# Two transposed loads on TensorE, six on-chip transposes, a shorter root, and a new instruction order in a one-core SSM + MLP kernel

## The chip, the cores and the metric

The kernel runs on one core of a Trainium2 chip. A core has five engines with an instruction queue each: TensorE (PE, matmuls; its weight loads are listed as PEld), VectorE (DVE), ScalarE (ACT), GpSimd (POOL) and SyncE (SP, which here only issues transfers). Transfers can be issued from SP, ACT and POOL; 16 DMA engines carry them. Operands lie in on-chip memory of 128 partitions; TensorE writes its results to a separate memory, PSUM, from which ACT or DVE must copy them out ("evacuate") before the space can be used again. The metric is device time in microseconds (us), the median of several runs.

## What is computed

Two layers, each an SSM convolution (A) and an MLP (B), on a sequence of 2048 tokens of 512 channels in bfloat16. Cut from the reference:

```
def _A_ref(q, k, v, shift_k, ssm_k, ssm_D):
    k_shift = causal convolution of k with 4 taps per channel (shift_k: 512 x 4)
    kv = k_shift * v
    y = causal convolution of kv with ssm_k over the sequence (FFT of length 2 S)
    return q * (y + kv * ssm_D)

def _B_ref(x, w1, b1, w2, b2):
    h = gelu(layernorm(x) @ w1 + b1)          # 512 -> 1376
    return h @ w2 + b2                        # 1376 -> 512

x = A_q
for layer in range(2):
    x = x + _A_ref(layernorm(x), A_k, A_v, A_shift_k, A_ssm_k, A_ssm_D)
    x = x + _B_ref(layernorm(x), B_w1, B_b1, B_w2, B_b2)
```

A's inputs k and v don't depend on x, so y is computed once and serves both layers.

## The kernel before

The sequence is cut into four groups of 512 tokens (j or g = 0 to 3). The convolution over the sequence is done blockwise in a transformed domain, all by matmuls with tables: K{j} is the transform of the filter's block j, U{j} that of kv's block j, and output block j is the inverse transform of the sum over a of U{a} times K{j-a}.

Work is cut into pieces, each added to a plan with a name and an engine. Two strings written out by hand fix everything: `ORDER` lists all pieces, each with its engine (S = SP, A = ACT, D = DVE, G = POOL, P0 to P3 = PE writing PSUM buffer 0 to 3), and the pieces of an engine stand in its queue in that order; `PLACE` gives each buffer its address in one large tile, `arena`, and four `zone` tiles. The names that matter below:

- Loads (line 324): lK{j} the filter's block, lk{j}, lv{j}, lx{j} the blocks of k, v and q, lT0 to lT3 the tables of the direct transform, lY the last table, ls the taps, lD the vector ssm_D, lb the bias b1, w1 and w2, w3, w4 the weights and b2. 
- KT{j} and kt{j} (lines 381, 402): 16 transposes on PE of the filter's or k's block, for j = 0 in two halves; KT00e is the evacuation of KT00, and so for all names with an e at their end. dt (line 386, DVE) adds ssm_D to the filter's first row.
- dg (line 362, DVE): turns the taps into 16 diagonal 64-wide matrices, with which kv{j}{h} (line 422) makes the 4-tap convolution on PE; kvm (line 433) multiplies it by v.
- KD, UD (line 459): the direct transform of blocks 0 and 1, eight matmuls of 128x512 each. KS and KW, US and UW (lines 484 and 493): the same for blocks 2 and 3 in two steps, with a regrouping through DMAs (Kx, Ux) between them. T (line 515, DVE): the products U times K. V, Vx, Y (lines 528, 324, 541): the inverse transform, again with a regrouping by DMA.
- For each layer l and group g, i = 2g + l: sa, pa, aa are the first norm's statistics (DVE, lines 274 to 281), root (POOL, lines 284 to 289) and application (ACT, line 294, or DVE, line 296); ga the gate and residual (lines 606 and 607); sb, pb, ab the second norm; then the normalized rows are transposed for the first product m1 (line 634, PE), whose result goes through the gelu ge (line 641, ACT), and m2 (line 652, PE) with its residual re (line 658, DVE) ends the layer; st (line 666) stores.

The transpose between ab and m1 has three ways: i = 0 goes through PE (LT, line 592); i = 7 by four DMA transposes that read on-chip memory (line 598, one per 128 tokens); all others write the rows to DRAM (dw, line 324, to a tensor `lnd`), and one DMA transpose reads them back (line 622).

The taps, the bias and ssm_D are loaded from POOL's queue: the taps as 512 pieces of four elements, the bias one element to a partition (lines 557 and 558), so that they land with channels in partitions.

In the built program every transfer of SP and ACT signals its landing on one of eight semaphores, DMAHW0 to DMAHW7, which are handed out in turn. A transfer that gets a semaphore for the second time waits before it is issued until the earlier transfer with that semaphore has landed.

Of the kernel before, what the change touches and what calls it, by code (L numbers as in the profile page):

```python
# [9 lines left out]
BF16 = mybir.dt.bfloat16  # L10
# [11 lines left out]
UD03e.A KD11.P0 aa22.D kt10e.A T001.D V00.P2 KD13.P1 KD11e.D V00e.A ke2.G ke3.G lF.A T002.D V01.P3 kv20.P2 V01e.A T003.D
V02.P0 kv21.P3 Vx01.S kvm20.D V02e.A Vx00.S V03.P0 kvm21.D kv10.P2 V03e.A Vx02.S US21.P3 kvm10.D KT20.P0 US21e.A Vx03.S
KD13e.D US20.P2 kv11.P3 ks100.S US20e.A KT20e.D US23.P1 Ux21.A KD12.P2 ks101.S kvm11.D US23e.A Ux20.S Y00.P0 US22.P3
KD12e.D Y00e.A KS22.P1 Ux23.S UD11.P2 US22e.A ga00.D KS22e.A Ux22.S T100.D Y01.P0 UD10.P3 Y01e.A ks110.S UD11e.A UD12.P1
ga02.D ks111.S UD10e.A sb00.D lK3.S UW23.P0 w1.S KS21.P2 UD12e.A UD13.P3 T110.D UW23e.A pb00.G KS21e.A on0.G UW20.P1
KS23.P0 UD13e.A UW20e.D KS20.P2 KS23e.A ab00.D UW21.P3 UW22.P1 KS20e.A sb02.D KT30.P0 UW22e.A Kx20.S V11.P2 KT30e.D
pb02.G UW21e.A LT00.P1 Kx22.S T101.D V10.P0 LT00e.A Kx21.S KS30.P3 V11e.A KS33.P1 V10e.A Kx23.S T111.D KS32.P2 KS30e.A
Vx11.S KS31.P0 KS33e.A ab02.D V13.P3 Vx10.S KS32e.A KS31e.D V12.P1 V13e.A LT02.P2 V12e.D KW23.P0 Vx13.S LT02e.A KW20.P3
T210.D KW22.P1 KW20e.A m103.P2 Vx12.S KW23e.A lk3.S KW21.P3 KW22e.D m105.P0 ge03.A w2.S KW21e.D m100.P1 ge05.A T221.D  # L30
ks201.S Y11.P2 Y10.P0 ge00.A m104.P3 ks200.S Y10e.A Y11e.D Kx32.S m101.P1 ge04.A T220.D Kx31.S m102.P0 ge01.A ga20.D
kt30.P2 ge02.A m200.P3 sb20.D Kx30.S Kx33.S kt30e.D pb20.G T200.D m202.P1 ab22.A ab20.A dw22.S re00.D T201.D dw20.S
V20.P0 T211.D V21.P2 V20e.A dr2.S kv31.P3 V21e.A re02.D KW31.P0 KW32.P2 KW31e.A lv3.S sa10.D V22.P1 KW32e.A V23.P0
sa12.D pa10.G V22e.A KW30.P2 m121.P1 on2.G V23e.D KW30e.A pa12.G aa10.A kvm31.D Vx23.S m125.P2 kv30.P0 aa12.D Vx21.S
ge25.A KW33.P3 ge21.A m122.P2 kvm30.D Vx20.S KW33e.A ga10.D US31.P1 Vx22.S ge22.A m124.P0 US31e.A sb10.D m120.P3 ge24.A
Ux31.S Y21.P2 ks300.S Y20.P1 ge20.A m123.P0 Y20e.D pb10.G Y21e.A US33.P3 ge23.A US30.P2 ab10.D US32.P1 ab12.D dw10.S
US32e.A m222.P0 ga40.D dw12.S US33e.A Ux32.S US30e.A Ux33.S sb40.D dr1.S m220.P1 T321.D Ux30.S pb40.G ks301.S ab42.A
T320.D ab40.A dw42.S m114.P3 re20.D dw40.S m113.P2 lx3.S ge14.A re22.D UW33.P1 m112.P3 T310.D ge13.A UW33e.A dr4.S
UW31.P0 m115.P2 sa32.D UW31e.A m110.P1 ge15.A T311.D ge12.A pa32.G UW30.P0 m111.P2 ge10.A sa30.D UW30e.A m145.P3 UW32.P1
m140.P0 ge45.A T301.D pa30.G UW32e.A m144.P3 aa30.A T331.D ge40.A m141.P1 ge11.A T300.D m142.P0 ge41.A V32.P2 T330.D  # L40
aa32.A V33.P1 V32e.A sa60.D ge44.A V31.P2 V33e.A V30.P3 ge42.A Vx33.S ga30.D pa60.G Vx32.S on1.G m143.P1 V30e.A on4.G
aa60.D V31e.A Vx30.S aa62.D m212.P0 sb30.D Vx31.A ge43.A pb30.G Y31.P3 Y30.P2 re12.D m240.P1 Y31e.A ab30.D Y30e.D ab32.D
ga60.D dw32.S dw30.S m210.P0 sb60.D dr3.S m242.P3 pb60.G re10.D st12.S on6.G ab62.A ab60.D dw62.S dw60.S m133.P2 re42.D
re40.D m135.P0 ge33.A m134.P3 dr6.S sa50.D m132.P1 sa52.D ge34.A pa50.G st10.S m131.P2 aa50.A pa52.G ge32.A m163.P3
aa52.D ga52.D ge35.A m165.P1 ge63.A ga50.D m130.P0 ge31.A sb50.D m164.P3 ge30.A sb52.D pb50.G ge65.A m161.P2 on3.G
pb52.G m162.P0 ge61.A ab52.D ge64.A m160.P1 ab50.D dw52.S dw50.S ge62.A m230.P2 ge60.A dr5.S m262.P3 re30.D st30.A
# [9 lines left out]
TD3:720 Dc:64 DG:1544 Ktok0:0 Ktok1:352 Ktok2:496 Ktok3:304 kT0:312 kT1:48 kT2:312 kT3:1158 K0:998 K1:560 K2:0 ziK2:1416
zsK20:16 zsK21:0 zsK22:336 zsK23:1528 K3:304 ziK3:1416 zsK30:416 zsK31:1319 zsK32:1335 zsK33:368 U0:1255 U1:1191 U2:432
ziU2:1352 zsU20:216 zsU21:0 zsU22:312 zsU23:16 U3:216 ziU3:1416 zsU30:1335 zsU31:934 zsU32:720 zsU33:736 ziV0:1416
T000:816 vs00:480 T001:0 vs01:280 T002:216 vs02:32 T003:416 vs03:264 y0:1576 x0:784 ziV1:1352 T100:32 T110:934 vs10:1560
vs11:1480 T101:720 T111:32 vs12:966 vs13:982 y1:496 x1:688 ziV2:1352 T200:1352 T210:304 T220:1480 vs20:1560 vs21:1335  # L60
# [642 lines left out]
```

## Time and profile before

| | us |
|---|---|
| median of 3 runs | 256.19 (254.76, 256.19, 256.83) |
| the profiled execution | 255.47 |
| its span, first to last instruction | 253.8 |
| DVE busy | 178.4 (70%) |
| ACT busy | 141.3 (56%) |
| POOL busy | 46.3 (18%) |

All times below come from that one profiled execution. Busy time is the time in which an engine has at least one instruction under way. In lists of groups, "x16" is the count of instructions; in a timeline a row is a run of like instructions, with the start, the time from the first's start to the last's end, and in square brackets how long the engine had been idle before it and what ended that. "SPq" and "ACTq" are the queues' own instructions, such as the issue of a transfer. Six of the eight DMA transposes of the MLP stage are those of line 622; one more group of four is line 598's.

### The profile page before, as it was taken

How to read it: one execution, taken by the hardware profiler on the slowest of the kernel's cores; microseconds unless marked ns; L12 is line 12 of the kernel's file. 1: busy time of each engine (PE TensorE's matmuls, PEld its weight loads, DVE VectorE, ACT ScalarE, POOL GpSimd, SP SyncE). 2: the span in 40 equal slices, each digit the busy share in tenths (PEclk: the TensorE clock that was granted, in tenths of full speed). 3: DMA queues.
4: the chain of work that ended last, by engine and by line, in shares of the span. 5: the costliest groups of instructions: out<-in, count | busy, mean ns of one | idle time of the engine just before them, and what ended most of it. 6: DMA issues, size and time to landing. Idle time of an engine off the chain costs nothing.

```text
span 253.8 us, 4351 instructions
## 1 busy us (share of the span) xinstructions
PE 240.5 (95%) x1675; PEld 115.4 (45%) x1675; DVE 178.4 (70%) x282; ACT 141.3 (56%) x184; POOL 46.3 (18%) x81
## 2 busy tenths in 40 slices
PE   2599999999999999999999999999999999999994
PEld 2354646434444545444444454444444444444452
DVE  0369898898999989899997995975870249630033
ACT  2428786679986347886298974121776044605400
POOL 7051300004000101210726041030230013300000
PEclk9999999999999999999999999999999999999999
DMA  6999954777669995466963015256205100211113
GB/s 195 232 259 284 295 166 112 201 194 301 189 155 302 182 209 129 147 164 182 212 187 63 3 30 140 83 124 164 45 18 147 41 3 1 53 30 41 44 31 94
DMA packets 37173, 34.59 MB, mean 136 GB/s; under 512 B 17408, under 2 KB 32896, under 8 KB 36896
## 3 DMA queue, kind: packets, MB, share of 16 engines
q1 hardware_dynamic: 34928, 32.06, 48.6%
q10 hardware_dynamic: 1904, 1.89, 3.1%
q0 software_dynamic: 320, 0.37, 0.7%
q8 instruction: 13, 0.21, 0.3%
q14 instruction: 8, 0.07, 0.1%
HBM read 12.80 MB, written 5.24 MB: 71 GB/s over the span
## 4 chain that ended last, share of the span: by engine, by line
PE 76%; DMA 8%; DVE 7%; POOL 3%; issue 2%; SPq 2%; ACT 2%; DVEq 0%; POOLq 0%
PE p L634 27%; PE p L652 23%; PE p L459 11%; PE p L528 6%; DMA zone<-arena 5%; PE p L484 3%; DMA arena<-in_A_ssm_D_dram 3%; SPq L324 2%; PE p L541 2%; PE p L493 1%; PE p L422 1%; DVE arena L658 1%; DVE arena L515 1%; DVE lst L274 1%; DVE arena L257 1%
## 5 line engine op out<-in xcount | busy, mean ns | idle before, releaser
L634 PE MATMUL p<-arena 128*128 128x512 bf16 (+1 forms) x352 | 78.9, 379 | 0.3 <-ACT arena L641 0.3
L652 PE MATMUL p<-arena 128*128 128x512 bf16 (+2 forms) x363 | 77.4, 372 | 0.1
L641 ACT ACTIVATE arena<-p,B 128x512 bf16<-128x512 f32 (+1 forms) x88 | 54.2, 684 | 41.0 <-PE p L634 39.7
L255 ACT ACTIVATE arena<-p 128x1024 bf16<-128x1024 f32 (+2 forms) x59 | 60.2, 1053 | 25.9 <-PE p L459 7.8
L284 POOL TENSOR_TENSOR lrs<-lrs,mhalf 128x2 f32<-128x2 f32 (+1 forms) x24 | 24.4, 1018 | 162.9 <-DVE lrs L278 86.4
L652 PEld LDWEIGHTS <-arena 128*128 128x128 bf16 (+1 forms) x363 | 35.3, 98 | 41.0 <-issue 0.8
L634 PEld LDWEIGHTS <-arena 128*128 128x128 bf16 (+1 forms) x352 | 34.4, 100 | 41.8 <-issue 3.5
L658 DVE TENSOR_TENSOR arena<-p,arena 128x1024 bf16<-128x1024 f32 (+2 forms) x19 | 19.8, 1053 | 46.4 <-PE p L652 46.4
L274 DVE BATCH_NORM_STATS2 lst<-arena 128x6 f32<-128x512 bf16 x64 | 40.2, 680 | 0.3
L515 DVE TENSOR_TENSOR arena<-arena 128x4096 bf16<-128x4096 bf16 (+1 forms) x16 | 32.0, 2017 | 1.4 <-ACT arena L255 1.2
L459 PE MATMUL p<-arena 128*128 128x512 bf16 x128 | 30.8, 395 | 0.5 <-DVE arena L386 0.5
L294 ACT ACTIVATE arena<-arena,lnm,lrs 128x512 bf16<-128x512 bf16 x24 | 18.0, 804 | 21.9 <-POOL lnm L289 21.9
L459 PEld LDWEIGHTS <-arena 128*128 128x128 bf16 x128 | 12.5, 101 | 16.5 <-issue 3.7
L528 PE MATMUL p<-arena,Mt 64*64 64x512 bf16 x224 | 14.9, 380 | 0.5 <-DVE arena L658 0.4
L515 DVE TENSOR_TENSOR zone<-arena 128x4096 bf16<-128x4096 bf16 x6 | 13.6, 2284 | 1.4 <-DMA zone<-arena 1.4
L296 DVE TENSOR_SCALAR arena<-arena,lmv,lrs 128x512 bf16<-128x512 bf16 x32 | 12.0, 424 | 2.5 <-POOL lrs L284 2.5
L528 PEld LDWEIGHTS <-Mt 64*64 64x64 bf16 x320 | 9.0, 106 | 8.9 <-issue 1.9
L257 DVE CAST arena<-p 128x1024 bf16<-128x1024 f32 x9 | 10.9, 1219 | 2.1 <-PE p L493 0.7
L257 DVE COPY arena<-p 128x2048 bf16<-128x2048 bf16 (+1 forms) x5 | 5.6, 1114 | 8.1 <-PE p L381 8.1
L381 PE MATMUL p<-IDt,arena 128*128 128x128 bf16 x64 | 5.1, 242 | 5.1 <-DMA arena<-in_A_ssm_k_dram 5.1
L484 PE MATMUL p<-arena,Ft 128*128 128x512 bf16 x40 | 9.8, 380 | 0.0
L255 ACT ACTIVATE zone<-p 128x1024 bf16<-128x1024 f32 x6 | 6.0, 1024 | 6.3 <-issue 3.5
(56 smaller groups left out, 138.2 us busy)
## 6 DMA issues: line engine op xcount, KB each, us to landing
zone<-arena SPq DMA_DIRECT2D x50, 128.0 KB, 2.5
lnd<-arena SPq DMA_DIRECT2D x12, 256.0 KB, 2.4
arena<-in_A_ssm_k_dram SPq DMA_DIRECT2D x4, 512.0 KB, 5.6
arena<-in_A_k_dram SPq DMA_DIRECT2D x4, 512.0 KB, 7.4
arena<-in_A_q_dram SPq DMA_DIRECT2D x8, 256.0 KB, 8.8
arena<-arena SPq DMA_DIRECT2D x8, 256.0 KB, 6.4
arena<-arena SPq DMA_DIRECT2D x14, 128.0 KB, 3.5
arena<-in_A_v_dram SPq DMA_DIRECT2D x3, 512.0 KB, 9.3
```

What stands on the lines that cost most here:

```text
L255: nc.scalar.activation(dst, src, AF.Copy)
L257: nc.vector.tensor_copy(dst, src)
L274: nc.vector.bn_stats(lst[:, i, :], xg[:, i, :])
L284: nc.gpsimd.tensor_tensor(self.rs[:, a:b], self.rs[:, a:b], mhalf[:, a:b], ALU.pow)
L294: nc.scalar.activation(dst[:, i, :], xg[:, i, :], AF.Identity, bias=self.nm[:, i:i + 1], scale=self.rs[:, i:i + 1])
L459: nc.tensor.matmul(o[:, r, :], at(f"TD{i}", (n * 2 + r) * P, [[1, P]]), at(src, n * D, [[1, D]]), start=n == 0, stop=n == 3)
L515: e.tensor_tensor(at(t, 0, [[2 * D * w, 2], [1, 2 * D * w]]), at(f"U{a}", 2 * i * D, [[0, 2], [1, 2 * D * w]]), at(f"K{kk}", 2 * i * D, [[ ...
L528: nc.tensor.matmul(o[64 * r:64 * r + 64, e, :], Mt[64 * e:64 * e + 64, 2 * i + r, s, :], at(f"T{j}{a}{i // TW[j]}", (s * 2 * TW[j] + 2 * ( ...
L634: nc.tensor.matmul(o[0:m, x, :], at("W1", ct * F + ft * P, [[1, m]]), at(LT, ct * 4 * P, [[1, 4 * P]]), start=ct == 0, stop=ct == CT - 1)
L641: nc.scalar.activation(at(HT, ft * 4 * P, [[1, 4 * P]], 0, m), o[0:m, x, :], AF.Gelu_apprx_tanh, bias=B1[0:m, ft:ft + 1])
L652: nc.tensor.matmul(o[:, x, c:c9], at(HT, ft * 4 * P + t * P, [[1, P]], 0, m), at("W2", ft * D + c, [[1, c9 - c]], 0, m), start=ft == 0, st ...
L658: nc.vector.tensor_tensor(xs, psum(pe, [2, D])[:, 0:len(tt), c:c9], xs, ALU.add)
```

## The change

There are six parts.

1. The taps are loaded as four rows of 512 elements (buffer `sr`, issued from ACT) and turned by four small PE transposes, sp, with an evacuation spe on DVE into the tile that dg reads.
2. b1 is loaded as 11 rows (issued from ACT in two transfers, after a memset bz on POOL), turned by one PE transpose, bp, and evacuated by bpe on ACT straight into the fp32 tile that the gelu reads; POOL's cast cb is gone.
3. lD is issued from ACT and w4 from SP; before, both were POOL's. lY, which led ACT's queue, now stands behind ls, lb and lD there.
4. `DIR` goes from {7} to {2, 4, 6, 7}: groups 1 to 3 of the first layer are turned by four DMA transposes each that read on-chip memory; their writes to DRAM are gone.
5. The factor -mean moves to the statistics (a DVE multiplication by -1, where ACT applies the norm), so that POOL's root is two operations and not three.
6. `ORDER` and `PLACE` are new. All pieces but those named have the same work; some evacuations and applications change between ACT and DVE.

```diff
 ORDER = """
-ls.G lT0.S lK0.S id.G lk0.S lY.A w4.G lx0.S lD.G lT1.S lv0.S lb.G lT3.S lT2.S KT01.P0 KT00.P1 KT01e.A ke0.G KT00e.D
+ls.A ke0.G lK0.S id.G lk0.S bz.G id2.D lb.A w4.S sp.P0 lT2.S lT1.S lD.A lY.A KT00.P1 bp.P2 KT01.P3 KT00e.A bpe.A KT01e.A
+lx0.S kt01.P1 dt.D spe.D kt00.P2 dg.D KD02.P0 lT0.S kt00e.A lv0.S kt01e.D lT3.S KD01.P3 lx1.S KD02e.A lx2.S sa02.D
...
-DIR={7}
+DIR={2,4,6,7}
...
-    b1T = const.tile([P, FT], BF16, name="b1T")
+    b1r = const.tile([FT, P], BF16, name="b1r")
...
+            if any(u["eng"] == "A" for c, u in uses):
+                nc.vector.tensor_scalar_mul(self.nm[:, a:b], self.mv[:, a:b, 0], -1.0)
...
-                nc.gpsimd.tensor_tensor(self.nm[:, a:b], self.mv[:, a:b, 0], self.rs[:, a:b], ALU.mult)
-                nc.gpsimd.tensor_scalar_mul(self.nm[:, a:b], self.nm[:, a:b], -1.0)
+                nc.gpsimd.tensor_tensor(self.nm[:, a:b], self.nm[:, a:b], self.rs[:, a:b], ALU.mult)
...
-        ls = load("ls", lambda: [(sT[:], A_shift_k.rearrange("(ct p) k -> p ct k", p=P))], engines="G", kb=[4])
+        ls = load("ls", lambda: [(at("sr", 0, [[1, P * KS]], 0, CT), A_shift_k.rearrange("(ct p) k -> ct (p k)", p=P))], engines="SAG", kb=[4], bufs=[buf("sr", P * KS)])
...
+        def taps(o):
+            for k in range(KS):
+                nc.tensor.transpose(o[:, k, :], at("sr", k, [[KS, P]], 0, CT), IDt[0:CT, 0:CT])
+        _, spe = mm_evac("sp", taps, [KS, CT], lambda: sT[:, :, :].rearrange("p c k -> p k c"), [ls, ident], 0.3, ["sr"], bf=True)
...
-        def bias(it):
-            nc.gpsimd.memset(b1T[:], 0.0)
-            nc.gpsimd.dma_start(b1T[:, 0:FT - 1], apf(B_b1, 0, [[1, P], [P, FT - 1], [1, 1]]))
-            nc.gpsimd.dma_start(b1T[0:FL, FT - 1:FT], apf(B_b1, (FT - 1) * P, [[1, FL], [1, 1]]))
-        lb = add("lb", "G", [], bias, us=2.5)
-        cb = add("cb", "G", [lb], lambda it: nc.gpsimd.tensor_copy(B1[:], b1T[:]), us=0.2)
+        b1z = add("bz", "G", [], lambda it: nc.gpsimd.memset(b1r[:, :], 0.0), us=0.2)
+        lb = load("lb", lambda: [(b1r[0:FT - 1, :], apf(B_b1, 0, [[P, FT - 1], [1, P]])), (b1r[FT - 1:FT, 0:FL], apf(B_b1, (FT - 1) * P, [[FL, 1], [1, FL]]))], [b1z],
+                  engines="SAG", kb=[2, 1])
+        _, cb = mm_evac("bp", lambda o: nc.tensor.transpose(o, b1r[:, :], IDt[0:FT, 0:FT]), [FT], lambda: B1[:, :], [lb, ident], 0.15, bf=True)
```

The first place is the start of ACT's queue, where the loads now stand. Of the names, Yt is the table of lY, sT the tile of the taps, b1r and B_75 the bias as rows and as it is used; p with a number is a PSUM buffer. Before:

```order
L324 DMA Yt<-tabY 128x64
L255 ACT_TABLE_LOAD
L255 ACTIVATE arena<-p_139 128x1024 [waits PE_49]
L255 ACTIVATE arena<-p_141 128x4x2x128 [waits PE_49,Pool_49]
L255 ACTIVATE arena<-p_142 128x4x2x128 [waits PE_49,Activation_49]
```

Now:

```order
L325 DMA arena<-in_A_shift_k_dram 4x512
L325 DMA b1r<-in_B_b_dram 10x128 [waits DMAHW0_49,Pool_49]
L325 DMA b1r<-in_B_b_dram 1x96 [waits DMAHW1_49]
L325 DMA arena<-in_A_ssm_D_dram 1x512 [waits DMAHW3_49]
L325 DMA Yt<-tabY 128x64 [waits DMAHW4_49]
L255 ACT_TABLE_LOAD
L255 ACTIVATE arena<-p_140 128x1024 [waits PE_49]
L255 ACTIVATE B_75<-p_141 128x11 [waits PE_49]
L255 ACTIVATE arena<-p_142 128x1024 [waits PE_49]
L255 ACTIVATE arena<-p_141 128x4x2x128 [waits PE_49]
```

ACT's first evacuation, which stood behind one transfer without a wait, now stands behind five transfers, four of which wait for a landing: DMAHW0, 1, 3 and 4 are those of ls, lK0, w4 and lT2.

The second place is SP's queue for the turning of the first layer's group 1 (i = 2). Before, two writes to DRAM and one transpose:

```order
L324 DMA zone_65<-arena 16x8x512 [waits DMAHW4_49]
L324 DMA lnd_130<-arena 128x2x512 [waits DMAHW5_49,DVE_49,Activation_49]
L324 DMA lnd_130<-arena 128x2x512 [waits DMAHW6_49,Activation_49]
L622 DMA_TRANSPOSE arena<-lnd_130 128x4x512 [waits DMAHW6_49,DMAHW7_49,DMAHW5_49,PE_49]
L324 DMA zone_66<-in_A_v_dram 128x2048 [waits DMAHW0_49,PE_49]
```

Now, with the load of v's block 3 between the two pairs:

```order
L603 DMA_TRANSPOSE zone_67<-arena 128x4x128 [waits DVE_49,PE_49,DMAHW2_49,Activation_49,Pool_49]
L603 DMA_TRANSPOSE zone_67<-arena 128x4x128 [waits DMAHW3_49,Activation_49]
L325 DMA zone_67<-in_A_v_dram 128x2048 [waits DMAHW7_49,DMAHW6_49,DMAHW4_49]
L603 DMA_TRANSPOSE zone_67<-arena 128x4x128 [waits DMAHW5_49]
L603 DMA_TRANSPOSE zone_67<-arena 128x4x128
```

The wait of SP's queue for the landing of its own two writes is gone; three issues have become four.

The third place is DVE's work around the products of block 1 (T of 128x4096) and the last evacuations before V13. Before, the last two products of block 1 stood ahead of the normalized rows of the second half and of four evacuations:

```order
L278 TENSOR_SCALAR lrs1_84<-lmv1_83 128x2
L257 COPY arena_63<-p0_139 128x2048
L515 TENSOR_TENSOR arena_63<-arena_63 128x4096 x2
L296 TENSOR_SCALAR zone2_66<-arena_63,lmv1_83,lrs1_84 128x512 x2
L257 CAST arena_63<-p0_139 128x1024
L257 CAST arena_63<-p1_140 128x1024
```

Now UW21e, T110, ab00, LT02e, V10e and the last product, T101, stand in a row:

```order
L257 CAST arena_63<-p2_141 128x1024
L521 TENSOR_TENSOR arena_63<-arena_63 128x4096
L297 TENSOR_SCALAR zone1_65<-arena_63,lmv1_83,lrs1_84 128x512 x2
L257 COPY zone3_67<-p3_142 128x4x256
L257 CAST arena_63<-p1_140 128x1024
L521 TENSOR_TENSOR arena_63<-arena_63 128x4096
```

The last product of block 1 moved behind an evacuation of LT (COPY) and one of V10 (the second CAST); V13 and V12 on PE read it.

More of the change, by code (lines that the diff above doesn't have):

```diff
@@ L22 @@
[L22 to L46, printed above, removed]
@@ L56 @@
[L56 to L60, printed above, removed]
```

67 lines of the change are left out of this document (48 added, 19 removed).

## The prediction

> **What bounds the kernel now.** I read the page's busy times first, then PE's own waits, then the timeline of the first 22 us.
>
> ```profile
> span 253.8 us, 4351 instructions
> PE 240.5 (95%) x1675; PEld 115.4 (45%) x1675; DVE 178.4 (70%) x282; ACT 141.3 (56%) x184; POOL 46.3 (18%) x81
> ...
> PE   2599999999999999999999999999999999999994
> ```
>
> PE is busy for 95%: of 40 slices of 6.3 us only the first two and the last show it idle. What is left to gain lies at both ends and in the waits between; here are all that the trace puts down to another engine or a transfer (total, times, longest):
>
> ```profile
> PE p L381 <- DMA arena<-in_A_ssm_k_dram: 5.1, 1, 5.1
> PE p L402 <- DMA arena<-in_A_k_dram: 2.6, 1, 2.6
> PE p L459 <- DVE arena L386: 0.5, 1, 0.5
> PE p L528 <- DVE arena L658: 0.4, 1, 0.4
> PE p L541 <- DMA zone<-arena: 0.3, 1, 0.3
> PE p L634 <- ACT arena L641: 0.3, 1, 0.3
> PE p L493 <- DVE arena L257: 0.3, 1, 0.3
> ```
>
> The first three are the start. The last four, 1.3 us together, are all the waits of some size in the other 240 us. So work moved between engines pays only through the start, the end and these four.
>
> ```profile
> 0.80 0.36 ACTq L324 DMA_DIRECT2D Yt<-tabY  x1
> 1.19 1.28 ACT L255 ACT_TABLE_LOAD   x1 [1.19 <-PEq L687]
> ...
> 5.05 1.89 PE L381 MATMUL p<-IDt,arena 128*128 128x128 bf16 x16 [5.05 <-DMA arena<-in_A_ssm_k_dram]
> ...
> 6.13 1.02 ACT L255 ACTIVATE arena<-p 128x1024 bf16<-128x1024 bf16 x1 [3.65 <-PE p L381]
> ...
> 9.51 1.89 PE L402 MATMUL p<-IDt,arena 128*128 128x128 bf16 x16 [2.56 <-DMA arena<-in_A_k_dram]
> ...
> 11.30 0.41 DVE L386 TENSOR_TENSOR arena<-arena 1x512 bf16<-1x512 bf16 x1 [3.36 <-DMA arena<-in_A_ssm_D_dram]
> ...
> 11.86 5.27 PE L459 MATMUL p<-arena 128*128 128x512 bf16 x16 [0.47 <-DVE arena L386]
> ```
>
> The first real product (KD00) starts at 11.86. ssm_D from POOL's queue came last, but only by 0.47 us: k landed at 9.5 and its transposes ended at 11.40. A load that is faster alone can thus win 0.47 us; the rest hangs on k.
>
> **The start, part by part.** Taps, b1 and ssm_D leave POOL's slow queue. The issues, in a window of the first 14 us (KB, median us to landing):
>
> ```profile
> GB/s 0 0 0 0 0 207 43 342 293 394 386 383 433 257 304 329 75 70 188 225 282 296 199 194 206 230 240 252 234 264 241 294 265 207 183 141 258 310 316 410
> ...
> Yt<-tabY ACTq DMA_DIRECT2D x1, 16.0 KB, 3.0
> ...
> arena<-in_A_ssm_D_dram POOLq DMA_DIRECT2D x1, 1.0 KB, 7.7
> ```
>
> From POOL 7.7 us, from ACT 3.0: ssm_D and the taps are no longer late. But the order puts lY behind them on ACT, with a wait for the landing of lT2 (call it T2), and the evacuation KT00e behind lY; the transposes kt01 need KT00e's PSUM buffer, and the first product, now KD02, stands behind both kt on PE. So KD02 starts at T2 plus lY's issue 0.36, the table load 1.28, KT00e 1.02, the kt transposes 1.89 and some 0.1 for four handovers: T2 + 4.65. That a transfer holds what stands behind it on ACT shows here:
>
> ```profile
> 154.05 1.20 ACTq L324 DMA_DIRECT2D zone<-arena  x2
> 155.30 1.27 ACT L641 ACTIVATE arena<-p,B 128x512 bf16<-128x512 f32 x2 [1.27 <-issue]
> ```
>
> The gelu, its input long done, started only after the two issues ahead of it. The Trainium skill ("DMA: Bandwidth & Descriptors", the section Anatomy of one DMA) says that any semaphore wait happens on the issuing sequencer before dispatch; the trace agrees with the 1.27 us. By that rule the move to ACT's queue costs what lT2's landing adds; were waits left to the DMA engines, the start would be that of the second rival.
>
> T2: ahead of lT2 on SP stand lK0 and lk0, with it 512 + 512 + 256 KB; before, lT0, lK0 and lk0 were the same 1280 KB, and k landed at 9.5. That is the late end. For the early end: the first 768 KB had landed at 5.05, and slices 8 to 16 of the window (0.35 us each) have a mean of 347 GB/s; the other 512 KB take 1.5 us at that rate, so 6.6. Between them lie the thin slices at 5.6 to 6.3 us (75 and 70 GB/s), while POOL's small pieces were under way. I take 7.15: the early end plus the 0.55 us that two such slices lose, in case they have another cause; nearer the early end, since those pieces are gone. KD02 then starts at 11.8 (bounds 11.25 and 14.15): **-0.1 us**, from -0.6 to +2.3.
>
> The five new transposes on PE (sp and bp) lie in PE's idle start. Their loads wait for at most lK0's landing and take 3.0 us more (about 7.4), so they are done before KT00e. No cost; with POOL's 7.7 us instead they would come at 12, and the start at the late end. spe and dg on DVE end before kv needs them.
>
> The first 16 products took 5.27 us, 16 later ones 3.56 (row below): 1.7 us for a slow clock at first. PE must start anew in the changed kernel too, so I carry the term over. "TensorE: Matmul & The Clock Gate" of the Trainium skill (Part 1) has the clock rise after one busy window of about 3.4 us that runs freely; by that rule the cold stretch may last up to twice as long from run to run, and cost as much as 1.7 us more. Two stretches of one trace can't show that.
>
> **On-chip transposes (groups 2, 4, 6).**
>
> ```profile
> lnd<-arena SPq DMA_DIRECT2D x12, 256.0 KB, 2.4
> ...
> arena<-lnd SPq DMA_TRANSPOSE x6, 4.4
> ...
> arena<-arena SPq DMA_TRANSPOSE x4, 2.5
> ```
>
> ```profile
> 217.89 5.11 SPq L598 DMA_TRANSPOSE arena<-arena  x4
> ```
>
> The way through DRAM takes 2.4 + 4.4 = 6.8 us after the last normalized row; two on-chip transposes take 1.28 of issue (5.11 / 4) and 2.5, so 3.8. That is 3.0 us earlier for m1, three times. But none of PE's waits above is for `lnd`, since m2 of an earlier group or V fills the time; I book **0**. On SP the four issues take 5.1 us, with regroupings (Vx, Ux) behind them. Group 1's last issue falls some 3 us ahead of Vx22's data, so they wait for nothing there; if it came late, Y21 on PE would wait.
>
> **The shorter root.**
>
> ```profile
> 120.92 4.49 DVE L515 TENSOR_TENSOR zone<-arena 128x4096 bf16<-128x4096 bf16 x2 [0.20 <-DMA zone<-arena]
> 121.88 1.39 POOL L288 TENSOR_TENSOR lnm<-lmv,lrs 128x4 f32<-128x4 f32 x1
> ...
> 123.36 2.15 POOL L289 TENSOR_SCALAR lnm<-lnm 128x4 f32<-128x4 f32 x1
> ...
> 125.54 2.93 ACT L294 ACTIVATE arena<-arena,lnm,lrs 128x512 bf16<-128x512 bf16 x4 [6.81 <-POOL lnm L289]
> ...
> 129.67 1.67 PE L634 MATMUL p<-arena 128*128 128x512 bf16 x7 [0.30 <-ACT arena L641]
> ```
>
> Here POOL's second and third operation took 1.39 and 2.15 us under DVE's products, ACT's rows came late, then the gelu, and PE lost 0.3 us. Without the 2.15 that wait goes (gain **0.3**, counted among the four). DVE gets 11 multiplications of 128x2 or 128x4 instead:
>
> ```profile
> L281 DVE TENSOR_SCALAR lrs<-lmv 128x2 f32<-128x2 f32 x10 | 2.1, 208 | 0.3
> ```
>
> At 0.2 us each that is 2.2 us spread over 200 on an engine that is busy for 70%; PE waits for DVE at one place only, which follows.
>
> **The new order's waits.** I laid the new order's PE sums against DVE's and ACT's and found one place where PE comes first: V13 needs T101, the last of a row of DVE work (place three of the change).
>
> ```profile
> L515 DVE TENSOR_TENSOR arena<-arena 128x4096 bf16<-128x4096 bf16 x12 | 27.2, 2284 | 1.4 <-ACT arena L255 1.2
> ...
> L296 DVE TENSOR_SCALAR arena<-arena,lmv,lrs 128x512 bf16<-128x512 bf16 x32 | 12.0, 424 | 2.5 <-POOL lrs L284 2.5
> L257 DVE CAST arena<-p 128x1024 bf16<-128x1024 f32 x9 | 10.9, 1219 | 2.1 <-PE p L493 0.7 <-PE p L541 0.5 <-PE p L528 0.5
> ...
> L257 DVE COPY arena<-p 128x1024 bf16<-128x1024 bf16 x1 | 0.7, 690 | 7.0 <-PE p L381 7.0
> ```
>
> From UW21's end DVE has UW21e 1.22, T110 2.28, ab00 2 x 0.42, LT02e 0.69, V10e 1.22, T101 2.28: 8.5 us, behind a lag of about 0.5 (ab02, just ahead).
>
> ```profile
> 63.98 0.55 PE p L592 x8
> ...
> 65.53 3.56 PE p L484 x16
> 69.09 1.88 PE p L528 x32
> ...
> 74.58 0.34 PE p L493 x4
> ```
>
> PE has four KS 3.56, two LT 1.10, V10 and V11 1.88, four W products 1.36: 7.9 us. V13 waits 8.5 + 0.5 - 7.9 = **+1.1** (0 if DVE has no lag and a faster product, 2.3 if it is a product later). The four old waits go: **-1.3** (half of it or none if like ones come back).
>
> **The end.** Before, the last store's halves were issued from SP and ACT; now both from SP, the second behind the first. The second half's landing moves by one issue at most: 0 if SP is free early and ACT was late before, 0.60 (half of the pair at 154.05) if not. I take **+0.4**, nearer an issue's own length.
>
> Sum: 253.8 - 0.1 + 1.1 - 1.3 + 0.4 = 253.9 of span, 255.6 for this execution (255.47 now). It lay 0.7 under the median of 256.19, so 256.3.
>
> **Rivals.** About 1%, 2.6 us, is what a measurement of this kernel can tell from no change.
>
> *Slower: lT2 lands late and ACT stays shut.* The price is 1 us of the end for each us of T2; at 9.5 the start is 14.15, and the sum 253.8 + 2.3 + 0.2 = 256.3, so 258.7 beside the median. It decides from T2 = 9.6 on. For it: the same 1280 KB did take until 9.5. Against: POOL's pieces are out of the rings. Chance of over 1% slower: 0.20.
>
> *Faster: ACT isn't held.* Then KT00e follows KT00 and PE's own row binds: lb at 7.4, KT01 and the kt to 10.25, so 1.6 us earlier; with no new wait at V13 the sum is 253.8 - 1.6 - 1.3 + 0.4 = 251.3, or 253.7 beside the median, at the border of 1%. Against it is the row at 155.30. Chance of over 1% faster: 0.14.
>
> *Nothing of it reaches PE*: the freed transposes and the root lie under PE's work, the start stays at k's landing, old waits come back elsewhere: 256.2 to 256.6. It can't be told from my forecast by the time. Together these two have 0.66, within 1%.
>
> **Numbers.** The likeliest: 256.3. Range: the faster rival's 253.7, and 258.7 of the slower one with some 0.5 us for the cold clock, 253.5 to 259.2.
>
> **What would show it.** Right: PE's first L465 product (the changed file's line of KD) at 11 to 12.5, with ACT's first evacuation 1.6 us behind lY's issue and lY's issue at lT2's landing; PE waiting for DVE's L521 by about 1 us near 70; no PE wait for a DMA transpose; POOL's lnm in one operation. Wrong: ACT evacuating before lY is issued; KD at 14; a PE wait of over 1 us anywhere else, above all for a transfer (Vx, Ux) behind the transposes on SP, or for w1, whose place in SP's queue is later.

## The result and the profile after

The changed kernel took **260.21 us** (median of four runs, 259.10 to 261.28), the kernel before 256.32 beside it; the ratio is 1.0145 with a 95% interval of 1.0100 to 1.0191. The forecast was 256.3, range 253.5 to 259.2, most likely within 1%. By this result it was wrong: slower by 1.45%.

The profiled execution took 261.28, 259.6 of it span (253.8 before). The page of the changed kernel (busy times, then slices of 6.5 us for PE and for the clock granted to it):

```profile
span 259.6 us, 4365 instructions
PE 241.2 (93%) x1680; PEld 115.7 (45%) x1680; DVE 179.6 (69%) x293; ACT 143.7 (55%) x186; POOL 36.9 (14%) x62
PE   2499999999793999999999999999999999999994
PEclk9999999999998699999999999999999999999999
```

There is a hole in the thirteenth slice, near 80 us, and the clock is lower in that slice and the next; before, both rows were full there. PE's waits on the changed kernel (total, times, longest):

```profile
PE p L564 <- DMA b1r<-in_B_b_dram: 4.4, 1, 4.4
PE p L547 <- issue: 4.1, 1, 4.1
PE p L372 <- DMA arena<-in_A_shift_k_dram: 2.4, 1, 2.4
PE p L387 <- DMA arena<-in_A_ssm_k_dram: 2.1, 1, 2.1
PE p L534 <- DVE arena L521: 1.4, 1, 1.4
```

Three are the start, in which PE idles anyway. L534 is V13, which waits for T101 as forecast. L547 is new: the first product of Y10. The rows around it, of PE's, SP's and ACT's timelines, with the issues of w2 on SP and of Vx12 on ACT:

```profile
73.50 1.81 ACTq L325 DMA_DIRECT2D zone<-arena  x2
73.57 0.60 SPq L325 DMA_DIRECT2D arena<-in_B_w_dram  x1
...
75.55 3.63 PE L639 MATMUL p<-zone,arena 128*128 128x512 bf16 x16
83.26 1.92 PE L547 MATMUL p<-zone,Yt 128*64 128x512 bf16 x8 [4.09 <-issue]
85.11 5.39 PE L639 MATMUL p<-zone,arena 128*128 128x512 bf16 x16
```

Sixteen products of m1 take 3.63 us ahead of the wait and 5.39 behind it. Y10 needs all eight transfers of Vx1 (the regrouping of V10 to V13, two each). The profile names "issue" as what ended the wait, so it doesn't say which transfer it was; the packets, further down, show the last of the eight still moving until about 82 us, and the edits below show that it counts.

I had the changed kernel timed twice more, unedited (the experiments f1 and g2):

| runs of the changed kernel | median | lowest to highest | kernel before beside them | runs over 258.5 us |
|---|---|---|---|---|
| first four | 260.21 | 259.10 to 261.28 | 256.32 | 4 of 4 |
| twelve more | 256.57 | 254.06 to 260.13 | 256.19 | 3 of 12 |
| twelve more | 257.72 | 254.48 to 261.86 | 255.98 | 6 of 12 |

The 28 runs fall into two groups, 15 from 254.06 to 257.07 and 13 from 258.61 to 261.86, with none between. The median of all is 256.97, against 256.04 in the 89 runs of the kernel before that the three sets of experiments have. Of those 89, 13 are over 258.5. All ratios here leave out runs over 1.5% above the kernel's fastest, so those of the two later rows (0.9987, 0.9945 to 1.0030, and 0.9978, 0.9935 to 1.0021) leave out just the upper group. So the change costs nothing measurable in one half of its runs and some 4 us in the other, and the first four were all of the second kind. Why all four were, I can't say. Since the kernel before has a few runs as long, not each long run has to have the wait of Y10; all three traces from the upper group do.

### The profile page after: what moved, and what is told of

Same layout as the page of the kernel before. It is cut to its first block, busy times and chain, and to the rows that moved or that the text cites. A ratio compares the mean times of both kernels' runs of the same rounds, so it can differ in the third digit from the quotient of the medians.

```text
span 259.6 us, 4365 instructions
## 1 busy us (share of the span) xinstructions
PE 241.2 (93%) x1680; PEld 115.7 (45%) x1680; DVE 179.6 (69%) x293; ACT 143.7 (55%) x186; POOL 36.9 (14%) x62
## 4 chain that ended last, share of the span: by engine, by line
PE 81%; DMA 8%; DVE 3%; issue 2%; ACT 2%; SPq 2%; DVEq 0%
PE p L639 30%; PE p L657 29%; PE p L465 8%; PE p L534 6%; DMA b1r<-in_B_b_dram 2%; PE p L428 2%; DVE arena L521 2%; PE p L408 2%; DMA zone<-arena 2%; PE p L547 2%; DMA arena<-in_A_ssm_k_dram 2%; ACT arena L255 1%; DMA Wt<-tabW 1%; DMA arena<-arena 1%; PE p L499 1%
## 5 line engine op out<-in xcount | busy, mean ns | idle before, releaser
L255 ACT ACTIVATE arena<-p 128x1024 bf16<-128x1024 f32 (+2 forms) x54 | 56.0, 1072 | 22.3 <-PE p L547 7.5
L639 PE MATMUL p<-arena 128*128 128x512 bf16 (+1 forms) x264 | 58.2, 379 | 0.0
L295 ACT ACTIVATE arena<-arena,lnm,lrs 128x512 bf16<-128x512 bf16 x22 | 16.5, 809 | 31.6 <-POOL lnm L290 24.5
L521 DVE TENSOR_TENSOR arena<-arena 128x4096 bf16<-128x4096 bf16 (+1 forms) x15 | 29.8, 2000 | 0.6 <-DMA zone<-arena 0.6
L465 PE MATMUL p<-arena 128*128 128x512 bf16 x128 | 29.5, 383 | 0.0
L639 PE MATMUL p<-zone,arena 128*128 128x512 bf16 (+1 forms) x88 | 22.2, 405 | 0.0
L534 PE MATMUL p<-arena,Mt 64*64 64x512 bf16 x240 | 16.0, 379 | 1.4 <-DVE arena L521 1.4
L297 DVE TENSOR_SCALAR arena<-arena,lmv,lrs 128x512 bf16<-128x512 bf16 x26 | 10.7, 462 | 5.8 <-POOL lrs L286 5.8
L255 ACT ACTIVATE zone<-p 128x1024 bf16<-128x1024 f32 (+2 forms) x12 | 12.9, 1096 | 2.1 <-PE p L499 1.4
L534 PEld LDWEIGHTS <-Mt 64*64 64x64 bf16 x320 | 8.7, 106 | 9.8 <-DVE arena L521 1.8
L611 DVE TENSOR_TENSOR arena<-arena 128x2048 bf16<-128x2048 bf16 (+1 forms) x8 | 7.6, 956 | 5.6 <-ACT arena L255 5.3
L521 DVE TENSOR_TENSOR zone<-arena 128x4096 bf16<-128x4096 bf16 x5 | 11.3, 2284 | 0.0
## 6 DMA issues: line engine op xcount, KB each, us to landing
arena<-in_A_q_dram SPq DMA_DIRECT2D x8, 256.0 KB, 5.6
arena<-arena SPq DMA_DIRECT2D x8, 256.0 KB, 6.2
```

Source lines behind the costliest of these rows:

```text
L255: nc.scalar.activation(dst, src, AF.Copy)
L295: nc.scalar.activation(dst[:, i, :], xg[:, i, :], AF.Identity, bias=self.nm[:, i:i + 1], scale=self.rs[:, i:i + 1])
L465: nc.tensor.matmul(o[:, r, :], at(f"TD{i}", (n * 2 + r) * P, [[1, P]]), at(src, n * D, [[1, D]]), start=n == 0, stop=n == 3)
L521: e.tensor_tensor(at(t, 0, [[2 * D * w, 2], [1, 2 * D * w]]), at(f"U{a}", 2 * i * D, [[0, 2], [1, 2 * D * w]]), at(f"K{kk}", 2 * i * D, [[ ...
L534: nc.tensor.matmul(o[64 * r:64 * r + 64, e, :], Mt[64 * e:64 * e + 64, 2 * i + r, s, :], at(f"T{j}{a}{i // TW[j]}", (s * 2 * TW[j] + 2 * ( ...
L639: nc.tensor.matmul(o[0:m, x, :], at("W1", ct * F + ft * P, [[1, m]]), at(LT, ct * 4 * P, [[1, 4 * P]]), start=ct == 0, stop=ct == CT - 1)
```

## The experiments

The theory: Y10's wait comes from the new place of Vx12. Before, the transfers of V1's rows were all issued on SP ahead of the 1280 KB of w2; now Vx12 is issued on ACT at the same time as w2, and its second transfer goes to the DMA engines behind w2's bytes. The wait of 4 us then brings the granted clock down for some 7 us. Rivals: ACT's queue is what is slow, whatever lies beside it; or Y10 waits for something other than Vx12; or the start, with b1's late load, is what costs the time.

The edits below are to the changed kernel's list of the order of work (name, engine, and for PE the buffer).

**Vx12 ahead of w2, on SP (e1).**

```diff
-ge05.A w2.S Vx12.A
+ge05.A Vx12.S w2.S
```

> The changed kernel, with one edit: Vx12 (the regrouping of V12 for group 1) is issued from SP ahead of w2's load, not from ACT behind it. Theory A (w2's 1280 KB ahead of Vx12 hold it up, so that Y10 on PE waits 4.1 us and PE's clock falls to half until 88.7): Vx12 lands within about 3 us of its issue, Y10's wait goes to under 0.5 us, the clock stays up, and the time falls by 5 to 7 us to 253.5 to 255.5. Theory B (ACT's queue itself is what is slow): the same here, since Vx12 leaves ACT; the next kernel tells them apart. Theory C (Y10 waits for another of the four regroupings or for ACT's evacuation): Y10 still waits 3 us or more, time 259 to 261. A wait of m200 for w2, which is issued 1.2 us later, may take back up to 1 us in each.

256.47 us (ten runs, 253.57 to 258.84), ratio 1.0020 (0.9972 to 1.0068). PE's waits in its profile:

```profile
PE p L564 <- DMA b1r<-in_B_b_dram: 3.9, 1, 3.9
PE p L372 <- DMA arena<-in_A_shift_k_dram: 2.3, 1, 2.3
PE p L387 <- DMA arena<-in_A_ssm_k_dram: 2.3, 1, 2.3
PE p L534 <- DVE arena L521: 1.4, 1, 1.4
PE p L639 <- DMA zone<-arena: 1.3, 1, 1.3
```

L547 is gone, and so is the fall of the clock; since only Vx12's issue was moved, Y10's wait was for Vx12. The time is above the 253.5 to 255.5 that I expected. A new wait of 1.3 us may be one reason: m125, the first product of group 1's m1, waits for its on-chip transposes. The changed kernel's trace doesn't have this wait, and neither has e3's below.

**Vx12 behind w2, on SP (e2).**

```diff
-ge05.A w2.S Vx12.A
+ge05.A w2.S Vx12.S
```

> The changed kernel with Vx12 issued from SP, but still behind w2's load. Theory A (the bytes of w2 ahead of it): Vx12 lands only after w2's 1280 KB, at 84 or later, Y10 waits 4 to 6 us, the time stays at 259 to 262. Theory B (ACT's queue is slow): Vx12 lands 3 to 5 us after its issue at 74, Y10's wait is under 1 us, the time 253.5 to 256.

One run: 263.09 us. Of PE's waits, the first:

```profile
PE p L547 <- DMA arena<-arena: 5.0, 1, 5.0
```

Off ACT's queue, but behind w2 on SP's, the wait is not shorter, it is longer. (The profile puts its end down to another transfer, but e1 and e2 differ only in whether Vx12 stands ahead of w2 or behind it.) So w2 ahead of Vx12 is enough for the wait. That ACT's queue is not slow by itself, the trace of e3 shows next.

**b1's turn behind KD01 (e3), and with Vx12 first (e4).**

```diff
-bp.P2 KT01.P3 KT00e.A bpe.A KT01e.A
+KT01.P3 KT00e.A KT01e.A
...
-KD01.P3 lx1.S
+KD01.P3 bp.P2 bpe.A lx1.S
```

> The changed kernel with the transpose of b1 (bp) and its evacuation moved on PE and ACT from between KT00 and KT01 to behind KD01. Theory S (b1's second transfer, landed at 10.06, holds KT01, the kt transposes and so KD02 on PE): KD02 starts at 11.2 to 11.6 where it was 12.83, time 1.0 to 1.5 us less, 258.7 to 259.2. Rival (ACT's first evacuation, held by lY's wait for lT2 until 8.5, binds alone): KD02 starts at 12.5 or later, time within 0.3 us of 260.2. Y10's wait stays in both.

> The changed kernel with both edits: Vx12 from SP ahead of w2, and bp behind KD01. If the two causes are separate and add (theories A and S): KD02 at 11.2 to 11.6, no wait of Y10, time 252.5 to 254.5, 2 to 3.5 us under the kernel before. Rival (the earlier start is used up by a longer wait for DVE at V13, which stands 1.4 us behind, or by m200's wait for w2): time as with the Vx12 edit alone, within 0.5 us.

e3: 257.40 us (253.54 to 260.76), ratio 0.9968 (0.9909 to 1.0026); e4: 256.28 (254.10 to 258.76), ratio 1.0035 (0.9996 to 1.0075). Ten runs each. e4 was expected at 252.5 to 254.5; its rival was right, that b1's later turn adds nothing to Vx12's edit. The start isn't where the time is lost. But e3 is the most telling trace of all: its order around w2 is that of the changed kernel, and its profiled execution is one of the lower group, with 252.8 us of span. Its issues and Y10:

```profile
73.56 1.51 ACTq L325 DMA_DIRECT2D zone<-arena  x2
73.62 1.45 SPq L325 DMA_DIRECT2D arena<-in_B_w_dram  x1
...
79.15 1.05 PE L547 MATMUL p<-zone,Yt 128*64 128x512 bf16 x8
```

No wait that the row shows (0.2 us by the list of waits), with Vx12 on ACT's queue as in the changed kernel: ACT's queue alone is not what is slow. The difference is in w2's issue: 1.45 us, where it was 0.60 in the changed kernel's profile, while ACT's pair was shorter, 1.51 for 1.81. Five traces of this order (the changed kernel's three, e3, and the halves below) show it alike: where w2's issue took 0.60, Y10 waited 3.8 to 4.1 us; where it took 1.39 or more, 0.3 at most. The packets of the changed kernel and of e3 fit this. First the changed kernel from 78 to 83 us, then from 75 to 79, by queue (q1 is SP's, q10 ACT's; packets, MB, share of 16 engines):

```profile
q1 hardware_dynamic: 871, 1.24, 96.5%
q10 hardware_dynamic: 144, 0.13, 10.6%
...
q1 hardware_dynamic: 951, 0.97, 92.4%
q10 hardware_dynamic: 118, 0.10, 12.2%
```

And e3, the same two windows:

```profile
q1 hardware_dynamic: 1031, 1.46, 105.9%
...
q1 hardware_dynamic: 789, 0.80, 65.1%
q10 hardware_dynamic: 264, 0.24, 25.3%
```

Vx12 is twice 128 packets of 1 KB and some small ones. In e3 ACT's queue is done before 78; in the changed kernel half of it moves after 79 us, and none from 77.5 to 79.5. Three windows of both kernels, the changed one first (PE, PEld, DVE, ACT, POOL busy, then granted clock, DMA share and GB/s):

```profile
72.00:79.00 7.00, 7.00 (x44) 2.82 (x36) 7.00 (x5) 5.33 (x8) 0.00 (x0) 1.00 0.97 254
79.00:84.00 5.00, 0.91 (x5) 0.42 (x6) 1.50 (x1) 1.27 (x3) 0.00 (x0) 0.79 0.95 221
84.00:92.00 8.00, 8.00 (x42) 3.52 (x39) 6.64 (x6) 3.56 (x5) 0.00 (x0) 0.70 0.94 175
...
72.00:79.00 7.00, 6.95 (x43) 2.83 (x36) 7.00 (x5) 5.33 (x8) 0.00 (x0) 1.00 0.86 251
79.00:84.00 5.00, 4.95 (x33) 2.35 (x33) 4.86 (x4) 3.69 (x7) 0.00 (x0) 1.00 1.07 260
84.00:92.00 8.00, 7.95 (x46) 3.92 (x45) 7.63 (x14) 2.33 (x4) 1.21 (x2) 1.00 0.97 165
```

The DMA engines are as busy in both; only whose bytes go first differs. PE stands for four of the five microseconds from 79 on, and the clock is at 0.70 in the eight behind.

**The changed kernel again (f1, g2).**

> The changed kernel itself, unedited, timed again beside the others. Theory: the wait of the first product of Y10 for the second transfer of Vx12 is not one fixed size; it stands between nothing and 5 us with the landing of that transfer beside the 1280 KB of w2, and where it is over about 3.4 us the granted clock falls to a half behind it. Then the runs spread over 252 to 260 us of span, those with the clock at 0.993 or under are the long ones, and the median is 257 to 260. Rival: the four first runs were what this kernel always takes, 259 to 261 in nearly all of ten, with a ratio of 1.01 to 1.02.

> The changed kernel unedited a third time, beside the halves. Theory: again both kinds of run, spans of 252 to 256 with the clock at 0.997 or over, and spans of 257 to 260, most of them with the clock at 0.992 or under; a quarter to a half of the runs are of the second kind. Rival: the long kind was the one chip of the first four runs and doesn't come back, or all runs are of it.

The numbers are in the table above. Both expected two kinds of run and both have them; f1's median is lower than expected, its upper group smaller. Both profiles are of the upper group and have the wait at the same place, 3.86 and 3.84 us, with w2's issue at 0.61 and 0.60. A mean clock under 0.9945 marks a run in which the clock fell in the middle: 10 of the 28 runs, and 2 of 10 in e3, but none of the 20 in e1 and e4, which have Vx12 ahead of w2. The mark alone doesn't say where it fell: 6 of the 89 runs of the kernel before have it too, and so do runs of f2, f3, f4 and g3 below, all with Vx12 first. Some of the upper group's runs have a higher clock; what they lost isn't seen without a trace.

**w2 in two halves (g1).** The transfer w2 keeps its place and loads rows 0 to 639 of 1280; w2b loads the others.

```diff
-ks200.S Y10.P3
+ks200.S w2b.S Y10.P3
```

> The changed kernel with w2 in two transfers of 640 KB, the second behind ks200 on SP; Vx12 stays on ACT behind the first. Theory: the second transfer of Vx12 goes to the DMA engines after the bytes of w2 that were issued ahead of it; at the 350 GB/s that the packets show there, 640 KB less land some 1.8 us earlier, so a wait of Y10 of 3.9 to 4.1 us becomes 0 to 2.3. Too short for the granted clock to fall: none or one of ten runs is below 0.994, where 5 of 16 runs of the changed kernel were; the longest span is under 257.5. What w2's second half is late for m200 takes up to 1 us of it back, in all runs. Rival: what delays Vx12 is ACT's queue itself, or memory that is slow in some runs; then long runs with a clock of 0.987 to 0.992 are as frequent as before.

256.13 us (254.76 to 262.02, twelve runs), ratio 1.0015 (0.9980 to 1.0050). One run of twelve is over 258.5 us and below a clock of 0.994, at 260.3 us of span, which is above the 257.5 that the theory gave as the longest; the other eleven lie under 257. So long runs were fewer with fewer bytes ahead, 1 of 12 beside 6 of 12 in the same set of runs; that fits the theory, but twelve runs are few. That the wait itself is shorter where it occurs isn't shown, since this profile has w2's long issue (1.39 us), and Y10 waits only 0.27. Still, here Vx12 didn't go ahead of w2's bytes as in e3: from 77.5 to 79.5 us ACT's queue moved 159 packets, nearly all of Vx12's second transfer, beside 433 of SP's. The second half costs m200 0.68.

**Group 1 of the first layer (i = 2) through memory again (f2)**, on e1. The expectation calls it group 2, by its i. Two writes (dw22, dw20) and one transpose (dr2) replace the four on-chip ones.

```diff
-dr22.S
+dw22.S
...
-dr20.S
+dw20.S dr2.S
...
-DIR={2,4,6,7}
+DIR={4,6,7}
```

> The kernel with Vx12 ahead of w2, and group 2 turned through memory as in the kernel before; groups 4 and 6 stay on-chip. Theory: the four on-chip transposes of group 2 are issued one after the other on SP, some 1.2 us each with the load of v's last quarter in their midst, so they land no sooner than the one through memory; m125's wait of 1.3 us stays within 1 us of that, and the time within 1 us of the 256.5 of the kernel with Vx12 first. Rival: the on-chip turn is what is late, the wait goes to zero and the time falls by 1.3 us or more.

259.16 us (257.05 upwards, twelve runs, one of them at 884.4, which stays unexplained), ratio 1.0141 (1.0097 to 1.0185). The wait that I expected to stay at 1.3 us is 3.3, the longest in mid-kernel:

```profile
PE p L639 <- DMA zone<-lnd: 3.3, 1, 3.3
...
95.21 0.35 SPq L325 DMA_DIRECT2D zone<-in_A_v_dram  x1
95.61 0.46 SPq L325 DMA_DIRECT2D lnd<-arena  x1
101.81 2.19 SPq L627 DMA_TRANSPOSE zone<-lnd  x1
```

Both the theory and its rival are wrong: in the new order the on-chip way is worth 2 us at this place, by one trace each, and more in time, since the clock fell for 3.4 us behind the longer wait (107.5 to 110.9 us). Part of it is v's load, which here stands ahead of the second write; in the kernel before it stood behind the transpose. How much, wasn't tried.

**KW23 and m105 ahead of V13 (f3)**, on e1.

```diff
-KW22e.D V13.P3 UW23e.A KW23.P1 V12.P2 V13e.A KW23e.D m105.P0 Vx13.S
+KW22e.D UW23e.A KW23.P1 m105.P0 V13.P3 KW23e.D V12.P2 V13e.A Vx13.S
```

> The kernel with Vx12 ahead of w2, and KW23 and m105 put ahead of V13 on PE. Theory: the 1.41 us in which PE waits for T101 are filled by KW23's 0.3 and m105's 0.87, and the wait shrinks to 0.2 to 0.4; the gap ahead of m125 takes some of it back (up to 1.0), since the transposes don't come sooner. Time 255 to 256.3, 0.2 to 1.3 less than with Vx12 first. Rival: V13's transfer Vx13 is on the path instead, Y10 waits by what V13 is later, and nothing is won.

258.05 us (256.03 to 260.43, twelve runs), ratio 1.0067 (1.0027 to 1.0107): slower than the 255 to 256.3 that I expected, and than e1's median. Of its PE waits, the three at this place:

```profile
PE p L499 <- ACT arena L255: 1.4, 1, 1.4
...
PE p L639 <- DMA arena<-in_B_w_dram: 0.6, 1, 0.6
PE p L534 <- DVE arena L521: 0.4, 1, 0.4
```

V13's wait falls to 0.4 as expected, but KW23 needs a PSUM buffer that ACT empties no earlier, and m105 then waits for w1's load. Three engines and a load come together at this point, so filling the hole with other work of PE doesn't help. And it costs the clock. Two stretches of 3.4 us, in the columns of the windows above:

```profile
69.20:72.60 3.40, 1.45 (x19) 0.66 (x11) 3.40 (x3) 2.72 (x3) 0.00 (x0) 1.00 0.89 252
72.60:76.00 3.40, 3.40 (x31) 1.21 (x33) 2.88 (x2) 0.64 (x1) 0.00 (x0) 0.50 0.48 159
```

None of the waits in the first is longer than 1.4 us, but together they leave PE busy for 43% of it, and in the second the clock is at a half. 8 of f3's 12 runs have a mean clock under 0.9945, none of e1's 10.

**PE kept busy at the start (f4, g3).** Vx12 first and b1's turn later, as in e4, and 38 products of the identity by itself into buffers that are not yet in use; nobody reads them.

```diff
+        for w, n in enumerate((14, 24)):
+            add(f"wm{w}", "P", [ident], lambda it, n=n: [nc.tensor.matmul(psum(it, [8, P])[:, x % 8, :], IDt[:], IDt[:], start=True, stop=True) for x in range(n)],
...
-sp.P0
+sp.P0 wm0.P3
...
-KT01.P3
+KT01.P3 wm1.P2
```

> The kernel with Vx12 ahead of w2 and b1's turn behind KD01, and 38 products of the identity by itself, that nobody reads, ahead of KT00 and behind KT01, where PE stood idle. Theory: the granted clock rises at the end of the first stretch of some 3.4 us in which PE is busy throughout; PE idle until 9.5 us puts the rise at 13 to 17, and kept busy from 2.5 it comes at 6 to 10. Then KD02 and the 15 products behind it take 3.6 to 3.8 us and not 5.3 to 5.6, kt01 and kt00 0.95 and not 1.9, and the time falls by 1.5 to 3 us against the kernel without these products (256.3), to 253 to 255. Rival: the clock rises at a time set by something else than PE's work, still at 13 to 17 us, and the time stays at 256.

> The kernel with the 38 products that nobody reads, Vx12 ahead of w2 and b1's turn behind KD01, unedited a second time. If the rise of the clock at 9 us is what made it 1.1% faster than the kernel before, it is again: 253 to 254.5 us, a ratio of 0.985 to 0.994. Rival: six runs were too few, and it is within 1%.

f4: **253.48 us** (six runs, 252.35 to 256.32), ratio 0.9886 (0.9828 to 0.9943). g3, the same kernel: **253.74** (twelve runs, 252.59 to 256.69), ratio 0.9934 (0.9898 to 0.9969). Both intervals are below 1, so this version beats the kernel before. The changed kernel, timed in the same set as g3, had a median of 257.72 (g2). The start of f4:

```profile
6.55 2.77 PE L378 MATMUL p<-IDt 128*128 128x128 bf16 x24
9.99 1.05 PE L412 MATMUL p<-IDt,arena 128*128 128x128 bf16 x16 [0.67 <-ACT arena L255]
10.88 3.62 PE L469 MATMUL p<-arena 128*128 128x512 bf16 x15
```

The transposes of k take 1.05 us, where e3 took 1.86, and KD's first products 3.62, where e3 took 5.30. In the trace the clock rises at 9.2 us here and at 7.0 in g3, where in e3 and e4 it rose at 14.6 and 16.8.

**The old root in that kernel (g4).** The norm's root in three operations on POOL again, DVE's multiplication by -1 taken out.

```diff
-            if any(u["eng"] == "A" for c, u in uses):
-                nc.vector.tensor_scalar_mul(self.nm[:, a:b], self.mv[:, a:b, 0], -1.0)
...
-                nc.gpsimd.tensor_tensor(self.nm[:, a:b], self.nm[:, a:b], self.rs[:, a:b], ALU.mult)
+                nc.gpsimd.tensor_tensor(self.nm[:, a:b], self.mv[:, a:b, 0], self.rs[:, a:b], ALU.mult)
+                nc.gpsimd.tensor_scalar_mul(self.nm[:, a:b], self.nm[:, a:b], -1.0)
```

> The kernel of the run just above, with the root of the norm in three operations on POOL as in the kernel before. Theory: the root on two operations is worth 0.3 us or less; the time is within 0.5 us of the run above, and POOL is busy some 8 us more in all. Rival: each norm's two ops stand on the path several times, and the time is over 1 us longer.

255.45 us (253.09 to 256.70, twelve runs), ratio 0.9996 (0.9961 to 1.0031), beside 253.74: 1.7 us more, where I expected 0.5 at most. The rival was right, as far as two intervals tell that overlap a little; the trace shows it better. Here g4, POOL, ACT and PE:

```profile
88.71 0.20 POOL L288 TENSOR_TENSOR lnm<-lmv,lrs 128x4 f32<-128x4 f32 x1
89.00 2.18 POOL L289 TENSOR_SCALAR lnm<-lnm 128x4 f32<-128x4 f32 x1
...
91.22 2.93 ACT L294 ACTIVATE arena<-arena,lnm,lrs 128x512 bf16<-128x512 bf16 x4 [7.93 <-POOL lnm L289]
...
95.96 1.06 PE L431 MATMUL p<-arena 64*128 64x256 bf16 x28 [0.86 <-ACT arena L255]
...
102.77 1.25 PE L642 MATMUL p<-zone,arena 128*96 128x512 bf16 x5 [1.22 <-DMA zone<-arena]
```

The third operation takes 2.18 us beside a product of DVE's. ACT's rows for group 1 come that much later, then kv31 waits 0.86 and m125 1.22 us, together about the 2.0 that the spans differ by (253.8 and 251.8). That m125's part is all the root's isn't shown, since e1 and e4, with the short root, wait 1.3 and 2.1 us there. In g3 neither wait is there:

```profile
89.28 2.93 ACT L295 ACTIVATE arena<-arena,lnm,lrs 128x512 bf16<-128x512 bf16 x4 [5.67 <-POOL lnm L290]
...
100.62 2.76 PE L643 MATMUL p<-zone,arena 128*96 128x512 bf16 x11
```

## Why the prediction was wrong, step by step

The terms of the sum beside what the profiled execution shows, in us:

| term | predicted | measured |
|---|---|---|
| first KD product | -0.1 | +1.0 (12.83 for 11.86) |
| its slow clock | carried over, 0 | -1.25 (4.02 for 5.27) |
| V13 for T101 | +1.1 | +1.41 |
| the four old waits | -1.3 | -1.28 |
| Y10 for Vx12 | none | **+4.09** |
| the clock behind it | none | **+2.6** (1.92 for 1.05, 5.39 for 3.63) |
| the end | +0.4 | +0.15 |

These make 6.7, the spans differ by 5.8; 0.9 I could not place. PE's idle time grew by 5.1, as its waits say, so the 0.9 lies in its busy time.

*The step that failed* is "I laid the new order's PE sums against DVE's and ACT's and found one place where PE comes first". The laying-out had engines in it, and no transfers. The new `ORDER` has `w2.S Vx12.A`, so Vx12 is issued on ACT just as w2 is issued on SP; the step of "The new order's waits" should have set Vx12's landing, with 1280 KB beside or ahead of it, against Y10. The trace before had the number for it: w2's issue at 75.22, and its 9.1 us from issue to landing, so 84.3.

```profile
arena<-in_B_w_dram SPq DMA_DIRECT2D x1, 1280.0 KB, 9.1
```

In the changed kernel Y10 is due 5.7 us after Vx12's first issue begins (73.50 and 79.17). The list of what would show the forecast wrong did name a wait for a Vx, but behind the transposes on SP, where none came. The rivals had no such case either.

*The price of a stall of this size* was missing too: the clock. The rows show 4.09 us of wait and another 2.6 behind it. In the Trainium skill, "TensorE: Matmul & The Clock Gate" (the section Why this matters for your kernels) asks for "No PE-idle gaps >~3µs between matmul bursts", since one such window puts the clock back to a half. The traces agree for the long waits: it fell after waits of 3.84 to 5.0 us at Y10, for 6.83 us, and in f2 for 3.41 after 3.3 us. But in f3 it fell, for 3.41 us, where no wait was over 1.4 us, and there the measurement decides.

*The start*: T2, taken at 7.15, was 6.76, and the chain behind it held to a tenth: lY's issue at 6.78, KT00e at 8.47, 1.7 us later. This is the better evidence that a wait for a landing holds ACT's queue: the row at 155.30 in the prediction shows a gelu behind two issues, not behind such a wait. What failed is "about 7.4" for b1's load:

```profile
4.75 5.30 DMA b1r<-in_B_b_dram
10.19 0.16 PE L564 MATMUL p<-IDt,b1r 11*128 11x11 bf16 x1 [4.37 <-DMA b1r<-in_B_b_dram]
12.83 4.02 PE L465 MATMUL p<-arena 128*128 128x512 bf16 x16
```

Its second transfer took 5.3 us, not 3.0, and bp stands ahead of KT01 and both kt on PE. The 1.0 us was given back by the clock, which rose at 13.6 us and not at 15.2. That the two nearly cancel is luck: with the same start the rise came anywhere from 12.3 to 15.4 us. With bp later (e3) KD02 starts at 11.17, but its first 15 products take 5.30, and they end at 16.47 beside 16.85: 0.4 us.

*On-chip transposes, "I book 0"*: nothing is seen of them against the kernel before, as forecast. The reason given, that m1 isn't late, held only for the old order; in the new one they carry 2 us (f2) and are just in time (e3, f4, g3), or late by 1.3 (e1) to 2.1 (e4).

*The shorter root, -0.3*: worth 1.7 by the medians (g4). The mechanism was the one described, a POOL operation of some 2 us beside DVE's products; it was priced at one place alone, near 123 us, and the new order has no slack for it at group 1's. So root and transposes do what they should, and the new order spends it.

*The old waits, V13, the end*: as forecast, within 0.3 us.

Without the stall the time is as forecast: the median of the lower 15 runs is 255.92, and e1 and e4 lie at 256.5 and 256.3. That is in part luck, since the start, its clock and the root each came out otherwise than the sum has them. That the first measurement was 1.45% slower is the stall, as far as its runs show it: the profiled one has it, and three of the four have a mean clock under 0.9945. What decides in a run whether w2's issue takes 0.60 or 1.39 us and more, and with it when Vx12's bytes go, stays open: in five traces the short issue and the wait go together, and none shows why.

## What to carry to other kernels

When an order moves transfers, lay them out like work of an engine: what bytes are issued ahead or at the same moment on any queue, and who needs the last packet. A small transfer that something waits for belongs ahead of a megabyte on the same queue, as in e1, not beside it on another; here its landing then depended on a race, and the times came in two groups. An idle PE at the start is worth filling: 38 products that nobody reads made this kernel some 2.5 us faster (253.5 and 253.7, where e4 without them took 256.3, in another set of runs with the kernel before at 255.8 beside it, and 256.2 and 256.0 beside the others). And short waits that come close together can bring the clock down as a long one does (f3).

## What the runs showed of the hardware

- A second queue is no sure way past a large transfer. In the window from 75 to 79 us of the changed kernel ACT's queue moved 118 packets, the end of Vx12's first transfer; its second, issued by 75.3 us, came from 79.5 us on, behind most of w2's bytes. In e3 both were through before most of w2's bytes, in g1 the second moved beside them. "DMA: Bandwidth & Descriptors" in the Trainium skill (Queues, rings and completion order) has each DMA engine alternate between the queues that have work, by packets of several descriptors. From 77.5 to 79.5 us g1's trace has both queues moving, which would fit; the changed kernel's has 655 packets of SP's queue and none of ACT's. Whether the second transfer's descriptors were late there or the engines took them late, the trace doesn't tell.
- The clock changes on a fixed raster. In the traces' records of the granted clock all the stretches between its changes inside the span are multiples of 3.413 us (68.27, 6.83 and 3.41 are 20, 2 and 1 of them), and the first rise comes anywhere from 12.3 to 15.4 us in the eight profiled executions that have the changed kernel's start. At half clock that spread of 3.1 us is up to 1.6 us from run to run, an estimate, and more than most of the terms above.
- The rise needs a raster's stretch that is nearly full of PE's work: with PE busy for about half of the stretch before (9.5 to 11.2 us in e3) the clock stayed, with 84% (e1) it rose. But 83% raised it in f1 (8.8 to 12.3 us) and not in f4 (2.4 to 5.8 us), so the border lies about there.
- The fall, too, goes by the share of such a stretch in which PE is busy, not by one wait: in six traces the stretches of mid-kernel behind which the clock fell had PE busy for 0 to 43% (43% in f3, above), and e1 and e4, with 61% (101.4 to 104.8 us) and 46% (102.2 to 105.6 us), kept the full clock.
